# Batch 0's last tokens of k and v: loads to 128 partitions, k spread by head with a mask

One core of a Trainium2 chip. The metric is the device time of one execution in microseconds (us), lower is better. Times in the text count from the start of the profiled execution. In lines of the profile, PE is TensorE (PEld its loads of weights), DVE is VectorE, ACT is ScalarE, POOL is GpSimd and SP is SyncE; L873 is line 873 of that kernel; "the chain of work that ended last" is followed back from the last instruction, at each step to what released it. A pair is two heads; pair 2 is heads 4 and 5.

## The reference

A linear attention without softmax, a norm, and then a gated feed-forward layer with a residual. Cut to what matters here:

```python
# q, k, v: [8 batches, 8 heads, 576 tokens, 64]
kv = np.einsum('bhsd,bhse->bhde', k, v)          # a sum over all 576 tokens
out = np.einsum('bhsd,bhde->bhse', q, kv)
rms = np.sqrt(np.mean(out * out, axis=-1, keepdims=True) + 1e-06)
x = out / rms * g_norm                           # to [4608 tokens, 512]
# then, for all tokens: gelu(x @ w_gate) * (x @ w_val) @ w_out, gated, plus x
```

The sum over tokens is what the change uses: k and v rows of a token may sit on any partition, as long as both sit on the same one. 576 tokens are 512 (4 on each of 128 partitions) and 64 last ones.

## The kernel before, the parts concerned

Batch 0 has to be loaded before anything can run. Its fp32 rows come over SyncE's queue, half of the heads at a time; tiles that are used later serve as landing places (`th_all` for the last tokens).

```python
def load_first_last(half):                        # last tokens of k and v, 4 heads
    hs = slice(half * HH, (half + 1) * HH)        # HH = 4
    for i, t in enumerate((k, v)):
        nc.sync.dma_start(
            out=first_raw[i][half][0 : R // 2, :].rearrange("p (h x) -> p h x", h=HH),   # 32 partitions
            in_=t[0, hs, M0:S, :].rearrange("h (p j) d -> p h (j d)", j=2),
        )
# order of the queue: q k | last k, last v | v (heads 0-3), q k (4,5) | last k, last v | v (4,5), q k v (6,7), weights
...
for t in first_last:
    nc.vector.memset(t, 0.0)                      # partitions 32 to 127 stay zero
...
def f_cast_last(i, half, copy):                   # fp32 to fp16, 32 x 512
    hs = slice(half * HH, (half + 1) * HH)
    copy(
        out=first_last[i].rearrange("p j h d -> p h j d")[0 : R // 2, hs, :, :],
        in_=first_raw[i][half][0 : R // 2, :].rearrange("p (h j d) -> p h j d", h=HH, j=2),
    )
...
def f_kv(pr):                                     # kv of a pair of heads, 128 x 128
    for j in range(NJ):
        nc.tensor.matmul(ps, lhsT=k16[:, j, cs], rhs=b16_t[0, "v"][...], start=(j == 0), stop=False)
    for j in range(2):
        kl, vl = (t[:, j].rearrange("p h d -> p (h d)")[:, cs] for t in first_last)
        nc.tensor.matmul(ps, lhsT=kl, rhs=vl, start=False, stop=(j == 1))
...
# the opening, in order; the last letter is the engine (A ScalarE, D VectorE, P GpSimd).
# kc, vc, qc: casts; lk, lv: casts of last tokens; kv: f_kv; kvo: its mask product;
# warm3: three matmuls of zeros that keep TensorE's clock up
opening = """
qc1P qc0A qT1 qT0 kc1P kc0A qo0D warm3 lv0D lk0P qo1A warm3 vc1D vc0A kv1 qc2A kv0 kvo1 kvo0 o1 kc2P qT2
lk1P lv1D sq1 qo2D o0 warm3 warm2 vc2P sq0 rd1 kv2 qc3P rt1 kvo2 rd0 ...
"""
```

## Time and profile before

| | before |
|---|---|
| time, median of 3 runs | 338.99 us (338.89 to 339.11) |
| span of the profiled execution | 337.3 us |
| TensorE busy | 326.6 us, 97% of the span |
| 512-byte packets of SyncE's queue in the opening | 512, all of them last tokens |
| v of heads 4 and 5 landed | 11.70 us |
| mask product of kv, pair 2, started | 12.95 us |
| first gelu started | 22.68 us |

TensorE is full from the first gelu on, so the table's last three rows are the whole case: a landing, the product that waits for it, and the point from which the rest has a fixed length (337.35 - 22.68 = 314.67 us; it is 314.61 to 314.67 us in all fourteen profiles of this case). "Landed" is the last of the sixteen completion increments that the trace holds for a transfer. The lines that carry this reading are in the prediction.

### The profile page before, as it was taken

How to read it: one execution, taken by the hardware profiler on the slowest of the kernel's cores; microseconds unless marked ns; L12 is line 12 of the kernel's file. 1: busy time of each engine (PE TensorE's matmuls, PEld its weight loads, DVE VectorE, ACT ScalarE, POOL GpSimd, SP SyncE). 2: the span in 40 equal slices, each digit the busy share in tenths (PEclk: the TensorE clock that was granted, in tenths of full speed). 3: DMA queues.
4: the chain of work that ended last, by engine and by line, in shares of the span. 5: the costliest groups of instructions: out<-in, count | busy, mean ns of one | idle time of the engine just before them, and what ended most of it. 6: DMA issues, size and time to landing. Idle time of an engine off the chain costs nothing.

```text
span 337.3 us, 6523 instructions
## 1 busy us (share of the span) xinstructions
PE 326.6 (97%) x2576; PEld 200.9 (60%) x2576; DVE 255.4 (76%) x498; ACT 161.5 (48%) x289; POOL 109.3 (32%) x127
## 2 busy tenths in 40 slices
PE   8889999999999999999999999999999999999993
PEld 3444454444844476447644674458444888788872
DVE  6755449669859988788677968796789877777754
ACT  3663384264335361536163535343454376646760
POOL 2783161990053108400650057003200251142232
PEclk9999999999999999999999999999999999999998
DMA  8999999669489272983498339924300330011004
GB/s 239 319 197 204 195 203 158 171 101 151 83 134 171 105 115 104 174 85 77 135 176 94 63 102 179 136 45 98 126 0 5 74 125 2 2 54 73 0 2 124
DMA packets 76688, 38.82 MB, mean 115 GB/s; under 512 B 42098, under 2 KB 74354, under 8 KB 76658
## 3 DMA queue, kind: packets, MB, share of 16 engines
q0 software_dynamic: 38752, 17.17, 40.4%
q1 hardware_dynamic: 37328, 20.71, 22.4%
q10 hardware_dynamic: 578, 0.52, 0.5%
q8 instruction: 20, 0.33, 0.4%
q14 instruction: 10, 0.08, 0.1%
HBM read 38.80 MB, written 9.44 MB: 143 GB/s over the span
## 4 chain that ended last, share of the span: by engine, by line
PE 90%; DVE 4%; DMA 3%; issue 0%; ACT 0%; POOL 0%; SPq 0%; DVEq 0%
PE gps L357 21%; PE vps L357 20%; PE wA L452 11%; PE rps L377 8%; PE fps L394 3%; PE Av L692 3%; PE Ag L692 3%; PE wE L452 3%; PE wD L452 3%; PE wF L452 3%; PE w L452 2%; DMA hid_s<-in_v_dram 2%; PE kvp L208 2%; PE Fv L692 2%; PE Fg L692 2%; DMA kf<-in_k_dram 2%
## 5 line engine op out<-in xcount | busy, mean ns | idle before, releaser
L345 ACT ACTIVATE ge<-gps 128x512 f16<-128x512 f32 x84 | 50.2, 598 | 98.4 <-PE gps L357 96.7
L357 PE MATMUL vps<-xT,wv 128*128 128x512 f16 x328 | 84.2, 379 | 0.8 <-DVE hid L346 0.8
L357 PE MATMUL gps<-xT,wg 128*128 128x512 f16 x328 | 84.3, 380 | 0.0
L346 DVE TENSOR_TENSOR hid<-ge,vps 128x512 f16<-128x512 f16 x84 | 57.4, 684 | 32.6 <-PE vps L357 28.7
L492 POOL TENSOR_TENSOR osb<-osb,t 128x512 f32<-128x512 f32 x28 | 35.3, 1277 | 138.0 <-DVE osb L488 132.4
L357 PEld LDWEIGHTS <-wv 128*128 128x128 f16 x328 | 32.1, 98 | 39.7 <-issue 1.1
L357 PEld LDWEIGHTS <-wg 128*128 128x128 f16 x328 | 30.7, 98 | 34.5 <-issue 0.2
L452 PEld LDWEIGHTS <-hid_s 128*128 128x128 f16 x384 | 37.6, 98 | 4.5 <-issue 0.2
L377 PE MATMUL rps<-wr,xT 128*128 128x512 f16 x144 | 32.5, 379 | 0.0
L452 PEld LDWEIGHTS <-hid 128*128 128x128 f16 x288 | 28.2, 98 | 5.5 <-issue 0.8
L386 ACT ACTIVATE th<-rps 128x512 f32<-128x512 f32 x36 | 21.5, 599 | 16.4 <-PE rps L377 16.4
L377 PEld LDWEIGHTS <-xT 128*128 128x128 f16 x144 | 14.1, 98 | 16.6
L245 DVE TENSOR_REDUCE ss<-sq 128x8 f32<-128x512 f32 x32 | 20.6, 680 | 2.9 <-ACT sq L243 2.8
L452 PE MATMUL wA<-wo_ts,hid_s 128*128 128x256 f16 x168 | 20.6, 273 | 0.0
L692 PEld LDWEIGHTS <-ws 128*128 128x128 f16 x192 | 18.8, 98 | 2.2
L391 ACT ACTIVATE th<-th 128x512 f32<-128x512 f32 x36 | 19.9, 623 | 0.0
L303 DVE TENSOR_TENSOR t<-op,ny 128x512 f16<-128x512 f32 x28 | 17.9, 685 | 0.1
L243 ACT ACTIVATE sq<-op 128x512 f32<-128x512 f32 x28 | 15.3, 598 | 4.5 <-PE op L226 4.1
L317 DVE TENSOR_TENSOR t<-t,g 128x512 f16<-128x512 f16 x36 | 15.4, 478 | 0.1
L425 DVE TENSOR_TENSOR hid_s<-hid 128x1536 f16<-128x1536 f16 x16 | 15.3, 954 | 0.2
L729 POOL TENSOR_TENSOR hid<-ge,c 128x512 f16<-128x512 f16 x6 | 7.0, 1163 | 23.4 <-ACT ge L723 23.4
L394 PE MATMUL fps<-wo,hid 128*128 128x512 f16 x48 | 11.2, 379 | 0.0
(172 smaller groups left out, 472.5 us busy)
## 6 DMA issues: line engine op xcount, KB each, us to landing
out_dram<-osb SPq DMA_DIRECT2D x14, 512.0 KB, 2.6
qraw<-in_q_dram POOLq DMA_DIRECT2D x7, 512.0 KB, 8.1
k<-in_k_dram POOLq DMA_DIRECT2D x7, 512.0 KB, 9.7
v<-in_v_dram POOLq DMA_DIRECT2D x7, 512.0 KB, 11.5
wg<-in_moe_w_gate_dram POOLq DMA_DIRECT2D x2, 512.0 KB, 8.2
wv<-in_moe_w_val_dram POOLq DMA_DIRECT2D x2, 512.0 KB, 9.0
wo<-in_moe_w_out_dram POOLq DMA_DIRECT2D x2, 512.0 KB, 13.6
out_dram<-osb SPq DMA_DIRECT2D x4, 256.0 KB, 2.9
```

Source lines behind the costliest of these rows:

```text
L245: nc.vector.tensor_reduce(out=out_, in_=sq, op=ALU.add, axis=mybir.AxisListType.X)
L303: nc.vector.tensor_tensor(out=t, in0=o, in1=scale, op=ALU.mult)
L345: nc.scalar.activation(out=ge, in_=gps, func=AF.Gelu)
L346: nc.vector.tensor_tensor(out=hids[blk][:, f, :], in0=ge, in1=vps, op=ALU.mult)
L357: nc.tensor.matmul(ps[:, j0 * P : j1 * P], lhsT=w[:, cc, :], rhs=xT_t[blk][:, j0:j1, cc, :], start=(cc == 0 and j0 == 0), stop=(cc == NP - ...
L377: nc.tensor.matmul(rps, lhsT=xT_t[blk][:, j, cc, :], rhs=wr16[:, cc, :], start=(cc == 0), stop=(cc == NP - 1),)
L386: nc.scalar.activation(out=th, in_=rps, func=AF.Tanh, scale=0.5)
L391: nc.scalar.activation(out=th, in_=th, func=AF.Copy, scale=0.5, bias=0.5)
L394: nc.tensor.matmul(fps, lhsT=hids[blk][:, f, j * P : (j + 1) * P], rhs=wo16[:, f, :], start=(f == 0), stop=(f == NF - 1))
L452: nc.tensor.matmul(ps[:, e - es[0], :], lhsT=a[:, f, e * P : (e + 1) * P], rhs=b[:, f, :], start=(start and e == es[0] and f == 0), stop=( ...
L492: nc.gpsimd.tensor_tensor(out=res_all[of], in0=res_all[of], in1=t_t[blk][of], op=ALU.add)
L692: nc.tensor.matmul(out_[:, r, :], lhsT=lhsT, rhs=rhs, start=(first and r == 0 and c == 0), stop=(c == 1), skip_group_check=True,)
```

## The change

Intent: load each pair of last rows to all 128 partitions, one head's two tokens (512 bytes) on each, instead of to 32 partitions with four heads on each. A row then belongs to head (partition mod 4). For k it is spread to four heads' columns and multiplied by a mask of rows (`of_head`, 1 where the row belongs to the head), so every matmul still sums only its own head's rows; v is copied twice, once for each head of a pair. The memsets of partitions 32 to 127 are no longer needed.

```diff
--- before.py
+++ after.py
@@ -789,14 +789,18 @@
     first_raw, first_last = [], []
     for which in "kv":
         t = hid_of[which]
-        first_last.append(t[:, 2 * H * NJ * D :][:, 0 : 2 * H * D].rearrange("p (j h d) -> p j h d", j=2, h=H))
-        first_raw.append([th_all[:, 2 * len(first_raw) + i, :] for i in range(2)])
+        rest = t[:, 2 * H * NJ * D :]
+        if which == "k":
+            first_last.append(rest[:, 0 : 2 * H * D].rearrange("p (j h d) -> p j h d", j=2, h=H))
+        else:
+            first_last.append(rest[:, 0 : 8 * D].rearrange("p (i j e d) -> p i j e d", i=2, j=2, e=2))
+        first_raw.append([th_all[:, 2 * len(first_raw) + i, 0 : 2 * D] for i in range(2)])
 
     def load_first_last(half):
         hs = slice(half * HH, (half + 1) * HH)
         for i, t in enumerate((k, v)):
             nc.sync.dma_start(
-                out=first_raw[i][half][0 : R // 2, :].rearrange("p (h x) -> p h x", h=HH),
+                out=first_raw[i][half],
                 in_=t[0, hs, M0:S, :].rearrange("h (p j) d -> p h (j d)", j=2),
             )
 
@@ -823,8 +827,6 @@
 
     zeros = consts.tile([P, C], FP16, name="zeros")
     nc.vector.memset(zeros, 0.0)
-    for t in first_last:
-        nc.vector.memset(t, 0.0)
     mask = consts.tile([P, P], FP32, name="mask")
     nc.vector.memset(mask, 0.0)
     nc.vector.memset(mask[0:D, 0:D], 1.0)
@@ -837,6 +839,10 @@
     nc.vector.memset(one32, 1.0)
     ident = consts.tile([P, P], FP16, name="ident")
     nc.vector.tensor_copy(out=ident, in_=ident32)
+    of_head = consts.tile([P, HH], FP32, name="of_head")
+    nc.vector.tensor_reduce(
+        out=of_head, in_=ident32.rearrange("p (r h) -> p h r", h=HH), op=ALU.add, axis=mybir.AxisListType.X
+    )
     grow32 = consts.tile([1, 2, D], FP32, name="grow32")
     nc.vector.tensor_copy(out=grow32, in_=grow[:, None, :].to_broadcast([1, 2, D]))
     grow16 = consts.tile([1, H, D], FP16, name="grow16")
@@ -877,12 +883,20 @@
                 in_=src.rearrange("p h (j d) -> p h j d", j=NJ)[:, hs, :, :],
             )
 
-    def f_cast_last(i, half, copy):
-        hs = slice(half * HH, (half + 1) * HH)
-        copy(
-            out=first_last[i].rearrange("p j h d -> p h j d")[0 : R // 2, hs, :, :],
-            in_=first_raw[i][half][0 : R // 2, :].rearrange("p (h j d) -> p h j d", h=HH, j=2),
-        )
+    def f_k_last(half, engs):
+
+        raw_ = first_raw[0][half].rearrange("p (j d) -> p j d", j=2)
+        for j, eng in enumerate(engs):
+            eng.tensor_tensor(
+                out=first_last[0][:, j, half * HH : (half + 1) * HH, :],
+                in0=raw_[:, j, None, :].to_broadcast([P, HH, D]),
+                in1=of_head[:, :, None].to_broadcast([P, HH, D]),
+                op=ALU.mult,
+            )
+
+    def f_v_last(half, copy):
+        raw_ = first_raw[1][half].rearrange("p (j d) -> p j d", j=2)
+        copy(out=first_last[1][:, half], in_=raw_[:, :, None, :].to_broadcast([P, 2, 2, D]))
 
     def f_qT(pr):
         q16 = b16_t[0, "q"].rearrange("p j h d -> p j (h d)")
@@ -903,7 +917,8 @@
                 ps, lhsT=k16[:, j, cs], rhs=b16_t[0, "v"][:, hs, j * D : (j + 1) * D], start=(j == 0), stop=False
             )
         for j in range(2):
-            kl, vl = (t[:, j].rearrange("p h d -> p (h d)")[:, cs] for t in first_last)
+            kl = first_last[0][:, j].rearrange("p h d -> p (h d)")[:, cs]
+            vl = first_last[1][:, pr // 2, j].rearrange("p e d -> p (e d)")
             nc.tensor.matmul(ps, lhsT=kl, rhs=vl, start=False, stop=(j == 1))
 
     def f_kv_out(pr):
@@ -981,8 +996,10 @@
         eng = rest[-1:]
         if name in ("qc", "kc", "vc"):
             f_cast(name[0], pr, engines[eng])
-        elif name in ("lk", "lv"):
-            f_cast_last("kv".index(name[1]), pr, engines[eng])
+        elif name == "lk":
+            f_k_last(pr, (nc.gpsimd if eng == "P" else nc.vector, nc.vector))
+        elif name == "lv":
+            f_v_last(pr, engines[eng])
         elif name == "warm":
             keep_warm(pr)
         elif name == "wg":
@@ -1022,8 +1039,8 @@
 
 
     opening = """
-    qc1P qc0A qT1 qT0 kc1P kc0A qo0D warm3 lv0D lk0P qo1A warm3 vc1D vc0A kv1 qc2A kv0 kvo1 kvo0 o1 kc2P qT2
-    lk1P lv1D sq1 qo2D o0 warm3 warm2 vc2P sq0 rd1 kv2 qc3P rt1 kvo2 rd0 kc3A qT3 wg1 wv1 ri1 o2 rt0 t1 warm3 warm1 sq2 vc3D
+    qc1P qc0A qT1 qT0 kc1P kc0A qo0D warm3 lk0D lv0P qo1A warm3 vc1D vc0A kv1 qc2A kv0 kvo1 kvo0 o1 kc2P qT2
+    lk1P sq1 qo2D o0 warm3 warm2 vc2P sq0 lv1A rd1 kv2 qc3P rt1 kvo2 rd0 kc3A qT3 wg1 wv1 ri1 o2 rt0 t1 warm3 warm1 sq2 vc3D
     rd2 qo3A xT1 kv3 wg2 wcg0P rt2 kvo3 ri0 ri2 warm2 o3 t2 xo1A wcg1P sq3a wcv0P sq3b g1 xT2 rd3a wcv1P rd3b
     wv2 t0 xo2A wg3 wv3 v1 xT0 rt3 ri3 xo0A g2 v2 t3a t3b xT3a xT3b g0 xo3aA xo3bD gelu v0 g3a v3a g3b v3b
     """
```

The prediction was made with this diff, the order of instructions that it builds to, and the profile of the kernel before.

> **What bounds the kernel now.** I read the page first, then the chain of work that ended last, then the transfers in stretches of time, then the timeline of the first 24 us. The page says where there is anything to win: TensorE is busy in nine tenths or more of every slice but the first three and the last (a slice is 8.4 us).
>
> ```profile
> PE   8889999999999999999999999999999999999993
> ```
>
> So only the opening, batch 0's attention up to about 22 us, can give time, and from there the work of TensorE simply follows: in the chain, TensorE runs without a gap above 0.03 us from 20.90 us through all the batches that I looked at (to 83 us). Whatever the opening gains should shift everything after it. In the opening the chain (start, length, what) runs through transfers:
>
> ```profile
> 1.27 5.13 DMA kf<-in_k_dram
> 6.40 0.02 issue
> 6.42 5.28 DMA hid_s<-in_v_dram
> 11.70 0.05 issue
> 11.75 0.62 POOL v L873
> 12.38 0.04 issue
> 12.42 0.38 PE kvp L902 x4
> 12.80 0.13 PE kvp L907 x2
> 12.93 0.02 issue
> 12.95 0.29 DVE kv L910
> 13.24 0.59 DVE ss L927
> ```
>
> The landing of v for heads 4 and 5 at 11.70 us sets it: GpSimd casts it, TensorE forms kv of pair 2, VectorE masks it, and from 12.95 us VectorE then works almost without a break to 18.19 us. So the question is when that v lands. It is the tenth transfer of one queue: q, k, last k, last v, v of heads 0 to 3, q, k of heads 4 and 5, last k, last v of heads 4 to 7, and then it. The transfers' view of four stretches (packets, bytes, mean rate; 5.50 to 7.00 us, 7.00 to 8.50, 9.25 to 11.00, 11.00 to 13.00) shows a queue that is busy throughout but moves half as much in two of them:
>
> ```profile
> DMA packets 376, 0.32 MB, mean 213 GB/s; under 512 B 18, under 2 KB 376, under 8 KB 376
> ```
> ```profile
> DMA packets 583, 0.57 MB, mean 379 GB/s; under 512 B 28, under 2 KB 583, under 8 KB 583
> ```
> ```profile
> DMA packets 456, 0.38 MB, mean 219 GB/s; under 512 B 32, under 2 KB 456, under 8 KB 456
> ```
> ```profile
> DMA packets 793, 0.76 MB, mean 382 GB/s; under 512 B 47, under 2 KB 793, under 8 KB 793
> ```
>
> The 512-byte packets are those of the last tokens. Each slow stretch begins when a pair of them has been started (4.75 to 6.2 us and 8.5 to 10 us by packet starts), and goes on into v's ordinary 1 KB packets, whose median rises from 46 ns to about 86 ns. v of heads 6 and 7, of the same form but behind no such pair, runs at full rate. The loss is 1.50 x (1 - 213/379) = 0.66 us and 1.75 x (1 - 219/382) = 0.75 us: 1.4 us in all, all ahead of the 11.70 us landing.
>
> **What the Trainium skill says.** "SBUF — State Buffer", section "Door 1: The DMA port swizzle", says that a transfer's rate depends on how many of 16 memory ports its partitions reach, and that partitions 0 to 31 reach 8, all 128 reach 16. The loads of last tokens go to partitions 0 to 31. The trace agrees in kind: 213 against 379 GB/s. It doesn't agree in amount: 128 KB at half rate would lose 128/200 - 128/380 = 0.3 us, an estimate from the two rates, where the trace loses 0.66 to 0.75. The congestion outlives the narrow packets. "DMA: Bandwidth & Descriptors", section "Why a DMA increments its semaphore by 16 and not by 1", says that the number of engines is the largest up to 16 that divides the slowest dimensions of both sides. That is 16 for 32 rows too, and the trace has sixteen completion increments for each narrow load, for the first from 5.80 to 6.96 us. So I read the words "over 16 engines" as no change of engines: if anything is won, it is from the partitions. "SBUF — State Buffer", section "Who interferes with whom", says that a VectorE instruction with two inputs in SBUF contends with a GpSimd instruction that reads SBUF. The new products are such; the kernel before has no test of it in this stage.
>
> **The change part by part.** Bytes, packets (512 B) and engines stay; only the destination's partitions change.
>
> 1. Transfers, on the path. If the slow stretches go, v of heads 0 to 3 lands 0.7 us earlier (8.49 to 7.8), v of heads 4 and 5 1.4 us earlier (11.70 to about 10.3), and k, v of heads 6 and 7 and the two weight pieces likewise.
>
> 2. Issues, beside. The queue's issues took 0.33 to 0.51 us each. The built program no longer gives the four narrow loads the mark of quick issue that they had; of unmarked issues of this queue the trace has four stores (L558), 0.60 to 0.73 us. So some 0.2 us more each: v of heads 0 to 3 would be issued at about 3.3 us instead of 2.82. Its packets need not begin before 5.5, and the first transfer went from issue (0.74) to first packets (about 1.8) in 1.1 us, so this is covered.
>
> 3. VectorE's first stage, beside. Two memsets of 0.48 us go, one reduction of 128x128 comes, about 0.25 us (the cast of that shape took 0.21). VectorE then waited 1.18 us for the transposes anyway: nothing gained.
>
> ```profile
> 1.19 0.48 DVE L827 MEMSET kf<- 128x512 uint32 x1
> ...
> 7.08 0.60 POOL L882 CAST kf<-th 32x512 f16<-32x512 f32 x1
> ...
> 7.44 0.52 DVE L882 CAST hid_s<-th 32x512 f16<-32x512 f32 x1 [0.27 <-DMA th<-in_v_dram]
> ...
> 10.93 0.60 POOL L882 CAST kf<-th 32x512 f16<-32x512 f32 x1
> ...
> 11.30 0.51 DVE L882 CAST hid_s<-th 32x512 f16<-32x512 f32 x1 [1.17 <-DMA th<-in_v_dram]
> ```
>
> 4. First half. One VectorE cast (0.52) and one GpSimd cast (0.60) become two products of 128x256 on VectorE and one spread copy of 128x256 on GpSimd. A VectorE product with 128x256 results takes 0.42 us (L941, 128x256 form), so some 0.38 each, 0.76 together; the copy about 0.35 (half of the 0.61 of 128x512, and a little). The products follow the copy of qT (ends 7.17) and end at about 7.95; the v cast follows, to 8.4 instead of 8.92. TensorE's keep-warm matmuls run to about 8.6 and hold kv of pair 1 there as well: it starts at 8.5 rather than 8.97. Of the 0.7 us that v wins here, about 0.45 arrives.
>
> 5. Second half. GpSimd's cast (0.60) becomes a product of half the elements (the 128x512 sum of L492 took 1.28, so about 0.65). VectorE's cast becomes one product (0.38), and v's copy moves to ScalarE (about 0.38, as its 128x256 square took). On ScalarE it stands behind two squares, which end about 0.45 earlier than 11.36, at 10.9; so it is done at 11.3. GpSimd casts v from 10.3 to 10.95. TensorE leaves its keep-warm matmuls at about 11.15. kv of pair 2 thus starts at about 11.15 and ends at 11.6 (before: 12.42 and 12.93), and its mask product starts at 11.7 instead of 12.95: 1.2 us won. VectorE has its qT copy and first reduction done by 11.1, so it isn't the bound there.
>
> 6. After that. VectorE's run from 12.95 to 18.19 us keeps its order and shifts. What it meets has moved as well: v of heads 6 and 7, the weight pieces, and the weights that GpSimd fetches from 12.95 us on, as its preceding work ends earlier. The weights of the later columns land some us ahead of their use, so TensorE doesn't meet a new wait.
>
> Sum: -1.2 us if the slow stretches vanish, of which nothing is lost later. 338.99 - 1.2 = 337.8.
>
> **The rivals.**
> (a) The slow stretches aren't from the 32 partitions but from the source, 16 KB per head read by all engines at once, or from 512-byte packets as such. Both stay as they are. Against it: the v packets behind the pair, with an ordinary source, are slow for almost a microsecond after the last narrow packet started, which looks like writes backing up. For it: the loss is twice what ports alone would give. Then v lands at 11.70 as before, the products are covered, and the time is 338.9 to 339.1.
> (b) The stretches only shrink. Each engine probably gets two source rows, hence eight neighbouring partitions, so at each moment several engines may still crowd one port. Half the gain, 338.4.
> (c) A new bound takes over: ScalarE's copy of v standing ahead of kv of pair 2, VectorE's two products ahead of the v cast, or products stretched by GpSimd's reads. Each adds 0.3 to 0.4 us where the transfers are early; it turns -1.2 into -0.8, 338.2. With (a) it gives 339.1 to 339.3.
> (d) The slower issues starve the engines: 0.2 to 0.5 us per pair, if descriptors of the changed form come late. Against it is the slack of about 2 us in part 2.
>
> **Range and chances.** I give the full mechanism about 55 in 100 (337.5 to 337.9), (b) and (c) some 25 (338.0 to 338.5), (a) and (d) some 20 (338.9 to 339.3). The middle of this is 337.9; eight in ten lie between 337.4 and 339.0. Two per cent are 6.8 us. The opening has 22 us, and the change touches under 2 us of its path, so neither limit is in reach: within 2% has 0.98.
>
> **What would show it.** Right: no stretch near 210 GB/s before 13 us; v of heads 4 and 5 landing at about 10.3; kv of pair 2 at about 11.2; the first gelu group (L345) at about 21.5 instead of 22.68; the rest of the span as long as before. Products near 0.38 us, narrow issues of 0.6 to 0.7 us. Wrong: slow stretches as before (the source, or packet size); early landings but a late kv of pair 2 with a wait on ScalarE or VectorE ahead of it (rival c); idle transfer engines between 5 and 10 us (rival d); or an opening that gains and a later wait of TensorE on weights that gives it back.

## The result

| | before | after |
|---|---|---|
| time, median of 4 runs | 339.05 us (338.89 to 339.24) | 338.48 us (338.47 to 338.61) |
| span of the profiled execution | 337.3 us | 336.6 us |
| v of heads 4 and 5 landed | 11.70 us | 10.85 us |
| mask product of kv, pair 2, started | 12.95 us | 12.22 us |
| first gelu started | 22.68 us | 21.94 us |

The result is correct, and 0.57 us shorter: ratio 0.9984, 95% interval 0.9967 to 1.0001. A ratio here is the mean time of one kernel's fast runs over that of the other's of the same rounds, so not quite the ratio of the medians. The change is too small for this interval to exclude that it does nothing, but the profiles agree with it. The intervals of two later measurements lie wholly below 1: the changed kernel again (e6_after_again) and, in the third group, the changed kernel with one tile padded (e10_pad64). What the opening won (0.73 us at the mask product, 0.74 us at the first gelu) stands to the end: 336.55 - 21.94 = 314.61 us is the same rest as before, to 0.05 us.

The transfers' view of the changed kernel, for three of the stretches that the prediction shows (5.50 to 7.00 us, 9.25 to 11.00, 11.00 to 13.00):

```profile
DMA packets 562, 0.51 MB, mean 338 GB/s; under 512 B 21, under 2 KB 562, under 8 KB 562
```
```profile
DMA packets 633, 0.60 MB, mean 341 GB/s; under 512 B 36, under 2 KB 633, under 8 KB 633
```
```profile
DMA packets 716, 0.70 MB, mean 350 GB/s; under 512 B 33, under 2 KB 716, under 8 KB 716
```

The slow stretches are gone: 338 and 341 GB/s where 213 and 219 were. But the third line was 382 before. The queue now runs a tenth slower everywhere behind the first loads of last tokens; its 1 KB packets take 51 ns in the median, where they took 46 outside the slow stretches. The chain of work that ended last, in the changed kernel (start, length, what):

```profile
4.33 5.34 DMA kf<-in_k_dram
...
9.72 0.22 POOL k L881
9.93 0.36 issue
10.30 0.78 POOL kf L890
11.08 0.57 POOL v L879
...
11.69 0.38 PE kvp L916 x4
...
12.22 0.29 DVE kv L925
```

It no longer goes through the landing of v at 10.85 us but through the one of k of heads 4 and 5 (9.67) and three pieces of GpSimd behind it: the cast of k, the new product for the last k (L890), the cast of v. So two things stand between the predicted 11.7 us and the measured 12.22: slower packets, and a GpSimd that is 0.2 us late. The timeline shows why the products of the second half were longer than I took them to be:

```profile
7.09 0.75 DVE L890 TENSOR_TENSOR kf<-th,of_head 128x256 f16<-128x256 f32 x2
...
9.72 0.62 POOL L881 CAST k<-kf 128x512 f16<-128x512 f32 x1 [2.49 <-DMA kf<-in_k_dram]
9.92 0.69 DVE L890 TENSOR_TENSOR kf<-th,of_head 128x256 f16<-128x256 f32 x1
...
10.30 0.78 POOL L890 TENSOR_TENSOR kf<-th,of_head 128x256 f16<-128x256 f32 x1
```

The two products at 7.09 us take 0.375 us each (0.75 for both), mostly with GpSimd idle. The one at 9.92 takes 0.69: it falls into GpSimd's cast of k. If VectorE waits until that cast ends (10.34) and then needs its 0.375, it ends at 10.7; it ended at 10.61. This is the contention that the Trainium skill states for a VectorE instruction with two inputs in memory against a GpSimd one that reads it ("SBUF — State Buffer", section "Who interferes with whom"). It struck whichever came second. Here GpSimd's product began while VectorE's was still running, and took 0.78 us. In e6_after_again, the same kernel again, GpSimd's began first and took 0.62; there VectorE's took 0.81, and ended 0.28 us after GpSimd's:

```profile
10.18 0.62 POOL L890 TENSOR_TENSOR kf<-th,of_head 128x256 f16<-128x256 f32 x1
10.27 0.81 DVE L890 TENSOR_TENSOR kf<-th,of_head 128x256 f16<-128x256 f32 x1
```

VectorE was free in time all the same: its mask product of pair 2 waited for TensorE (0.68 us), so on the chain only GpSimd's part counts.

### The profile page after: what moved, and what is told of

Its sections match the earlier page's. It is cut to its first block, busy times and chain, and to the rows that moved or that the text cites. A ratio compares the mean times of both kernels' runs of the same rounds, so it can differ in the third digit from the quotient of the medians.

```text
span 336.6 us, 6522 instructions
## 1 busy us (share of the span) xinstructions
PE 326.7 (97%) x2576; PEld 200.9 (60%) x2576; DVE 255.1 (76%) x498; ACT 161.5 (48%) x290; POOL 109.4 (33%) x127
## 4 chain that ended last, share of the span: by engine, by line
PE 91%; DVE 4%; DMA 2%; SPq 1%; issue 1%; POOL 0%; ACT 0%; DVEq 0%
PE gps L357 21%; PE vps L357 21%; PE wA L452 11%; PE rps L377 8%; PE fps L394 3%; PE Av L692 3%; PE Ag L692 3%; PE wF L452 3%; PE wE L452 3%; PE wD L452 3%; PE w L452 2%; DMA kf<-in_k_dram 2%; PE kvp L208 2%; PE Fg L692 2%; PE Fv L692 2%; PE op L226 1%
## 5 line engine op out<-in xcount | busy, mean ns | idle before, releaser
L386 ACT ACTIVATE th<-rps 128x512 f32<-128x512 f32 x36 | 21.5, 598 | 16.4 <-PE rps L377 16.4
```

The costliest lines, as they stand in the source:

```text
L386: nc.scalar.activation(out=th, in_=rps, func=AF.Tanh, scale=0.5)
```

## The experiments

Theory: the 32 partitions cause the slow stretches, and taking these away is the whole gain. Rivals: the gain comes of the new arithmetic (products, fewer memsets), or of the slower form of issue. Then two questions that the result opened: what makes packets slower, and what holds the opening now. Twelve kernels ran, in three groups of four; the first two groups on one chip, the third on another. Runs in the slow state (over 1.5% above the fastest of the same kernel; here one of the kernel before, 344.84 us) are left out of ratios.

### 1. The transfers alone (e1_dst128)

The kernel before, with only the destination changed. The casts keep engine, number and size; they read one head's 512 bytes four times over, so the result is wrong on purpose.

```diff
-                out=first_raw[i][half][0 : R // 2, :].rearrange("p (h x) -> p h x", h=HH),
+                out=first_raw[i][half][:, 0 : 2 * D],
...
-            in_=first_raw[i][half][0 : R // 2, :].rearrange("p (h j d) -> p h j d", h=HH, j=2),
+            in_=first_raw[i][half][0 : R // 2, 0 : 2 * D].rearrange("p (j d) -> p j d", j=2)[:, None, :, :].to_broadcast([R // 2, HH, 2, D]),
```

> The kernel before with nothing changed but the destination of the four loads of last tokens: 128 partitions of 512 bytes instead of 32 of 2 KB. The casts stay as they were in number, engine and size (they read one partition's 512 bytes four times over, so the result is wrong on purpose). If the partitions are the cause of the two slow stretches, both vanish as in the changed kernel (about 340 GB/s instead of 213 and 219), v of heads 4 and 5 lands near 10.9 us instead of 11.70, its cast on GpSimd starts near 11.0, the mask product of pair 2 near 12.1 to 12.2, and the time is 338.4 to 338.5, the whole gain of the change. If the gain came from the changed arithmetic (products, copies, memsets taken away), the time stays at 338.9 to 339.1 whatever the transfers do.

Measured, transfers from 5.50 to 7.00 us and from 9.25 to 11.00:

```profile
DMA packets 617, 0.57 MB, mean 377 GB/s; under 512 B 29, under 2 KB 617, under 8 KB 617
```
```profile
DMA packets 690, 0.66 MB, mean 378 GB/s; under 512 B 44, under 2 KB 690, under 8 KB 690
```

No slow stretch, and full-speed packets (46 ns). v of heads 4 and 5 landed at 10.26 us, against a predicted 10.3 for the changed kernel (and 10.9 expected here, after the changed kernel's profile), and the mask product started at 11.79, against a predicted 11.7:

```profile
11.79 0.29 DVE L910 TENSOR_TENSOR kv<-kvp,mask 128x128 f16<-128x128 f32 x1 [0.68 <-PE kvp L907]
```

So the destination alone does what the prediction gave to the whole change, and more than the whole change did (12.22). By times this batch decides nothing: 338.54 us (338.03 to 342.78, 6 runs) against 339.59 (338.67 to 344.84, 11 runs), ratio 0.9983, interval 0.9935 to 1.0031. The kernel before scattered on this chip; experiment 4 shows one such execution.

### 2. The form of issue (e2_form)

The kernel before, correct, its four narrow loads kept from the quick form of issue, the destination unchanged.

```diff
+        nc.dge_precook = False
         for i, t in enumerate((k, v)):
             nc.sync.dma_start(
...
+        nc.dge_precook = True
```

> The kernel before, right result, with the four loads of last tokens to 32 partitions as before but issued in the slower form that the changed kernel's loads have (the mark of quick issue withheld). Theory of the partitions: each of these issues takes about 0.6 us instead of 0.33 to 0.50, the slow stretches stay (near 215 GB/s), v of heads 4 and 5 lands at 11.7, and the time stays at 338.9 to 339.2. Rival, that it is the form or the later issue that keeps the queue from congesting: the stretches vanish here too and the time falls to about 338.5. Side question: whether packets of 1 KB take 51 ns instead of 46 after such loads, as in the changed kernel; if so that comes of the form.

Measured, same two stretches:

```profile
DMA packets 415, 0.37 MB, mean 248 GB/s; under 512 B 16, under 2 KB 415, under 8 KB 415
```
```profile
DMA packets 503, 0.46 MB, mean 263 GB/s; under 512 B 29, under 2 KB 503, under 8 KB 503
```

The slow stretches stay. They are milder than 213 and 219, but not milder than those of the kernel before on this chip (254 and 279, experiment 4). The four issues in this form took 0.59 to 0.76 us, v landed at 11.32, and the time was 339.06 us (338.67 to 339.45). The form costs nothing that shows, and isn't what helps. It isn't what slows the packets either: 46 ns.

### 3. Which 32 partitions, and 64 (e3_32apart, e9_64low)

Two variants of the kernel before, both wrong on purpose. The first puts the rows on 32 partitions four apart; the second on the 64 neighbours 0 to 63. The cut shows the destinations alone: e3 has four clearing memsets on GpSimd as well, e9 casts that fit its rows, and both the slower form of issue.

```diff
-                out=first_raw[i][half][0 : R // 2, :].rearrange("p (h x) -> p h x", h=HH),
+                out=first_raw[i][half].rearrange("(p s) (h x) -> p s h x", s=4, h=HH)[:, 0],      # e3
+                out=first_raw[i][half][0:R, 0 : 4 * D],                                           # e9
```

> The kernel before with the loads of last tokens put on 32 partitions four apart (0, 4, ... 124) instead of 32 neighbours; packets, rows per partition and the slower issue form included; GpSimd clears the tiles first, in its idle time; the casts read partitions 0 to 31 as before (wrong result on purpose). If the cause is which memory ports the partitions reach, these 32 reach all 16 and the slow stretches vanish: no 1 KB packets near 86 ns, v of heads 4 and 5 near 10.9 us, time 338.4 to 338.6. If it is the number of partitions, or four rows going to one partition, the stretches stay at about 215 GB/s and the time at 338.9 to 339.2.

> The kernel before with the loads of last tokens on the 64 neighbouring partitions 0 to 63, 1 KB each (the casts read 32 of them, wrong result on purpose). By the skill's map of memory ports, partitions 0 to 63 reach the same 8 ports as 0 to 31, so the slow stretches should stay much as they were (200 to 250 GB/s for 1 us or more, v of heads 4 and 5 near 11.3 to 11.7). If it is the number of partitions that counts, they shrink to about half, or vanish. Time 338.7 to 339.1 by the ports.

Measured from 5.50 to 7.00 us, first 32 partitions four apart, then 64 neighbours:

```profile
DMA packets 617, 0.57 MB, mean 380 GB/s; under 512 B 25, under 2 KB 617, under 8 KB 617
```
```profile
DMA packets 376, 0.34 MB, mean 228 GB/s; under 512 B 11, under 2 KB 376, under 8 KB 376
```

32 partitions suffice if they are spread, and 64 don't if they are neighbours from 0 on. In the second stretch the spread ones had 324 GB/s with a median of 46 ns (a few single packets of up to 0.55 us in it, none of the broad slowing), the 64 neighbours 243 GB/s. v of heads 4 and 5 landed at 10.15 and at 11.49 us. That is what the Trainium skill's map of ports says ("SBUF — State Buffer", section "Door 1: The DMA port swizzle"): 0 to 63 reach the same 8 of 16 as 0 to 31. The number of partitions, the rows per partition and the packet size don't explain it; the set of partitions does.

By times, 338.63 us (338.50 to 339.07, 4 runs) and 339.13 (338.74 to 339.80, 4 runs). The spread one expected 338.4 to 338.6 and lost some of its early landing: its profiled execution had the mask product only at 12.46 us. Experiment 7 is about why.

### 4. Both kernels again (e6_after_again, e7_before_again)

Unchanged copies, on the chip of the first group.

> The changed kernel, unchanged, on another chip and beside the kernel before again. Question: its 1 KB packets took 51 ns (345 GB/s) after the loads of last tokens, where the transfer-only version with the very same loads had 46 ns (382 GB/s) throughout. If that belongs to the changed kernel, it is there again; if it varies from execution to execution, it need not be. Second question: the full TensorE clock was granted at 8.43 us here and between 7.81 and 9.57 us in the other profiles; kv of pair 1 started with the end of the keep-warm matmuls, so I expect its start to follow that instant (about 0.35 us behind it when the grant comes after 8.1 us). Time 338.3 to 338.6.

> The kernel before, once more with a profile, on the chip of these runs. If the slow stretches are its own, they are there again: two of about 1.5 us at 200 to 250 GB/s, v of heads 4 and 5 at 11.3 to 11.7 us, against a version of the quick or slow issue form, which had 11.32. If they were a chance of one execution, they are missing.

The changed kernel: 338.40 us (338.35 to 338.64, 6 runs), packets at 49 ns, v landed at 10.73. Beside the kernel before of the two groups (12 runs, 339.3 in the median; 339.0 without the slow one), the ratio is 0.9962 (0.9928 to 0.9995). The ratio counts the long runs of the kernel before that aren't slow by the rule (up to 341.94 us), so it flatters the change. Its slower packets are its own, then, not a chance of one execution: on this chip five versions of the kernel before had 46 ns, and three of the changed kernel 49 or 51. One expectation was a miss: kv of pair 1 started at 9.06 us, ahead of the full clock (9.31) and not 0.35 behind it.

The kernel before: slow stretches again, 254 and 279 GB/s, as expected. But this execution took 340.31 us (a single run, so its state is unknown), and v of heads 4 and 5 landed at 12.54, outside what I expected. The completion increments show where: fifteen of the sixteen for v of heads 0 to 3 had come by 8.20 us, the sixteenth at 10.02, so one engine lagged. It did so from the first last k on (fifteen by 6.65, the sixteenth at 8.12). One 512-byte packet of 0.64 us stands at 5.81, but the trace doesn't name its engine, and it is shorter than the lag. From one such profile I can't say what makes an engine fall behind, nor that the change mends it (one of six runs of e1_dst128 took 342.78 us). So the kernel before's long runs on this chip are not counted as a gain of the change.

### 5. GpSimd's product moved, and v's copy brought forward (e5_k_dve, e8_v_first)

```diff
-    lk1P sq1 qo2D o0 warm3 warm2 vc2P sq0 lv1A rd1 ...
+    lk1D sq1 qo2D o0 warm3 warm2 vc2P sq0 lv1A rd1 ...          # e5
+    lk1D lv1A sq1 qo2D o0 warm3 warm2 vc2P sq0 rd1 ...          # e8
```

> The changed kernel with both products of the second half's k on VectorE, none on GpSimd. In the changed kernel the chain goes through GpSimd's cast of k (9.72), its product (10.30, 0.78 us) and then its cast of v (11.03, while v landed at 10.85). With the product gone, the cast of v starts on the landing, at about 10.9, kv of pair 2 at about 11.55 instead of 11.69, and the mask product near 12.05 instead of 12.22: 0.15 to 0.2 us off the changed kernel. Rival: VectorE's products wait while GpSimd's cast of k reads memory (its one product took 0.69 us there instead of 0.38), so two of them, the copy of qT and the reduction end at about 12.2 and nothing is gained.

> The changed kernel with both products of the second k on VectorE and the second copy of v on ScalarE moved ahead of the two squares. With the products moved alone, kv of pair 2 waited for GpSimd's cast (to 11.35) and then for ScalarE's copy, which stood behind the squares (11.12 to 11.53), and was masked at 12.01. Ahead of the squares the copy runs as it lands (9.9 to 10.35), so the mask product should start near 11.85, 0.15 us less again, if the squares (0.2 us later) do not become the bound through the reduction. Time 0.1 to 0.2 below the version with the products moved, 338.0 to 338.1. Rival: the delayed squares delay the first reduction and square root by as much, and nothing is won.

With both products on VectorE, the cast of v followed its landing (10.74 against 10.69), and the mask product started at 12.01 instead of 12.22 (12.35 in the second profile of the changed kernel): 0.2 us, as expected. Both products together took 0.84 us, part of it in GpSimd's cast, and VectorE was free in time. 338.18 us (338.12 to 338.57, 6 runs), ratio to the kernel before of its batch 0.9957 (0.9927 to 0.9988); against 338.40 of the changed kernel on the same chip, in another batch, 0.2 us less. Within a batch the times don't confirm this: the next version, which has the moved product too, took 338.47 us beside those 338.40, and e12_pad_k_dve 338.47 beside 338.52 of e10_pad64. So the 0.2 us is shown at the mask product, in single profiles, and not by times.

Bringing v's copy forward was a miss: mask product at 11.99, and 338.47 us (338.15 to 339.08). TensorE began kv of pair 2 at 11.46 us, with the end of GpSimd's cast, as it had in e5_k_dve (11.47), and then needs 0.53 us to the mask product. ScalarE's copy, which I took for the bound, had been ready in time in both.

### 6. The tile that moved the others (e10_pad64, e11_dst128_by32, e12_pad_k_dve)

The new tile `of_head` moves every tile behind it by 32 bytes, landing places included. First a mend (64 bytes), then the converse (32 bytes put into e1_dst128), and the mend together with the moved product.

```diff
-    of_head = consts.tile([P, HH], FP32, name="of_head")
+    of_head = consts.tile([P, 16], FP32, name="of_head")[:, 0:HH]      # e10 and e12
...
+    pad = consts.tile([P, 4], FP32, name="pad")                        # e11, in e1_dst128
+    nc.vector.memset(pad, 0.0)
```

> The changed kernel with its new tile of four numbers per partition (of_head) given 64 bytes instead of the 32 that it takes. In the changed kernel that tile moved every tile behind it by 32 bytes, so that none of the loads' destinations starts at a multiple of 64 bytes any more; in all four profiles with it 1 KB packets take 49 to 51 ns after the first loads of last tokens, in all six without it 46. If the alignment is the cause, they take 46 ns here (about 380 GB/s), v of heads 4 and 5 lands near 10.3 us instead of 10.7 to 10.85, the mask product of pair 2 starts near 11.9 to 12.0 (then after ScalarE's copy of v), and the time is 0.2 to 0.3 below the changed kernel: 338.1 to 338.3. If the slower packets come from the arithmetic (products, fewer memsets), they stay at 49 to 51 and the time at 338.4 to 338.5.

> The converse: the transfer-only version (old casts, 128 partitions, wrong result on purpose), which had 46 ns throughout, with a tile of 32 bytes put ahead of the others and cleared once. If the alignment is the cause, its 1 KB packets take 49 to 51 ns from the first loads of last tokens on, v of heads 4 and 5 lands near 10.75 instead of 10.26, and the time rises by about 0.4 us to that of the changed kernel (338.4 to 338.6). If not, nothing changes (46 ns, 10.26).

> The changed kernel with the 64 bytes and with both second products of k on VectorE: the two mends together. v lands near 10.3 and its cast on GpSimd no longer waits for a product, but kv of pair 2 then waits for ScalarE's copy of v behind the squares (to about 11.4 to 11.5), so over the 64 bytes alone I expect no more than 0.1 us: 338.0 to 338.2.

The mend failed: 51 ns, v landed at 10.82, 338.52 us (338.43 to 339.12). The converse came as expected; its transfers from 11.00 to 13.00 us, where e1_dst128 had 373 GB/s:

```profile
DMA packets 713, 0.70 MB, mean 349 GB/s; under 512 B 32, under 2 KB 713, under 8 KB 713
```

51 ns, v at 10.74, 338.56 us (338.39 to 339.04, 5 runs). A multiple of 64 bytes is therefore not enough. It could be the place as such: in the kernel before, the places for q and v start at multiples of 256 bytes, and neither shift keeps that. But the two answers came from the other chip, where no version with the old places was profiled. Either the places do it, or the new arithmetic on one chip and something of the other chip on the other. The traces set a limit to the places as well. In every version with moved places, packets of the first q and k, which go to moved places too, take 46 ns in the median until about 4.5 us; only from the first loads of last tokens on do packets take longer. And in e1_dst128 the place for k starts 64 bytes past a multiple of 256 (by the built program's addresses), and they take 46 ns throughout. So a moved place alone doesn't slow a packet, nor do the new loads alone; in these runs the slowing shows only where both are present. What slows the packets stays open; only the theory "a multiple of 64 restores it" has fallen.

e11_dst128_by32 bears on another point. It has the changed kernel's transfers at their slower rate and none of its arithmetic, and takes 338.56 us beside 338.52 of the changed kernel with 64 bytes, on the same chip; both beat the kernel before of that batch (339.07 us, 338.89 to 339.67, 9 runs), with ratios 0.9985 (0.9972 to 0.9997) and 0.9983 (0.9969 to 0.9996). So the new loads make the gain without the new arithmetic, which is there to make the loads usable. What the arithmetic adds or takes is too small for these times: the medians differ by 0.04 us, and each version's five runs spread over 0.65 to 0.7. e12_pad_k_dve: mask product at 12.04, as in e5_k_dve (12.01), since the places gave nothing; 338.47 us (338.17 to 338.94), ratio 0.9978 (0.9966 to 0.9991).

### 7. The keep-warm matmuls (e13_fewer_warm)

In profiles with an early v, kv of pair 1 started at quite different times, 8.45 to 9.21 us. The six matmuls of zeros ahead of it are the same in all; their lines in the timelines of e8_v_first, the changed kernel and e6_after_again (start, length):

```profile
6.50 1.87 PE L858 MATMUL idle<-zeros 128*128 128x512 f16 x6
```
```profile
6.51 2.41 PE L858 MATMUL idle<-zeros 128*128 128x512 f16 x6
```
```profile
6.50 2.77 PE L858 MATMUL idle<-zeros 128*128 128x512 f16 x6
```

The trace's first record of TensorE's full clock is at 7.32, 8.43 and 9.31 us in these three. Until then a matmul of 512 columns starts every 0.43 us, later every 0.22. The Trainium skill says so: the clock is gated to half until TensorE has been busy for one window of about 3.4 us, and the window runs freely, so the instant differs from run to run ("TensorE: Matmul & The Clock Gate", section "Part 1: The HAM clock gate"). It names a spread of 0.5 us either way; the fourteen profiles here have 7.32 to 10.10 us. In the profile of the kernel before this didn't matter, as the clock came at 7.83, v landed at 8.47 and was cast by 8.92. It is no matter of the new loads alone: in e2_form, with the old destination, v was cast by 8.71, and with the clock at 9.57 kv of pair 1 started at 9.06. With v at 7.7 to 8.2 the matmuls of zeros are what kv of pair 1 waits for whenever the clock comes late. The last experiment drops two of them, on top of e12_pad_k_dve.

```diff
-    qc1P qc0A qT1 qT0 kc1P kc0A qo0D warm3 lk0D lv0P qo1A warm3 vc1D vc0A kv1 ...
+    qc1P qc0A qT1 qT0 kc1P kc0A qo0D warm3 lk0D lv0P qo1A warm1 vc1D vc0A kv1 ...
```

> As the version with both mends, and the last group of keep-warm matmuls ahead of kv of pair 1 cut from three to one. With the full clock granted at 8.4 us or later these matmuls ended only at 8.7 to 9.2 us and held kv of pair 1, whose v was cast by 8.5. If they are the bound, kv of pair 1 starts at about 8.4 whatever the grant, the squares and ScalarE's copy of v come up to 0.5 us earlier, the mask product of pair 2 starts near 11.7, and the time falls by 0.1 to 0.3 us to 337.8 to 338.0. Rival: with fewer of them the full clock comes later, and the matmuls and transposes until then run slower: no gain or a loss.

The profiled execution had a late clock, 9.79 us. Its keep-warm matmuls and kv of pair 1 in the timeline, and then those of e10_pad64 with nearly the same instant (9.88):

```profile
6.50 1.91 PE L858 MATMUL idle<-zeros 128*128 128x512 f16 x4
8.62 0.59 PE L916 MATMUL kvp<-v,k 128*128 128x128 f16 x4 [0.21 <-DVE v L879]
```
```profile
6.50 2.77 PE L858 MATMUL idle<-zeros 128*128 128x512 f16 x6
9.06 0.63 PE L916 MATMUL kvp<-v,k 128*128 128x128 f16 x4
```

kv of pair 1 now waits for v, not for zeros, 0.44 us earlier, and the mask product of pair 2 starts at 12.21 instead of 12.57. That compares two kernels that differ in the moved product too (0.2 us). It does not reach the 11.7 that I expected, nor the time the 337.8 to 338.0: at half clock, kv itself is slow, and v had landed at 8.12. 338.33 us (338.18 to 338.47, 5 runs), ratio 0.9974 (0.9961 to 0.9986). Beside e12_pad_k_dve (338.47 us) the median is 0.14 lower, and the spread is 0.3 us instead of 0.8. With five runs that is a hint, not a verdict. The rival, a later clock for want of matmuls, isn't excluded: 9.79 us is the third latest of the fourteen, from one profile.

### All in one table

Times in us. "Full clock" is the trace's first record of it; "1 KB" is the median time of a 1 KB packet of SyncE's queue from 10.9 to 13.5 us; n is the number of runs.

| version | full clock | kv pair 1 | v 4, 5 landed | mask pair 2 | first gelu | 1 KB, ns | median (n) |
|---|---|---|---|---|---|---|---|
| before | 7.83 | 8.97 | 11.70 | 12.95 | 22.68 | 46 | 339.05 (4) |
| after | 8.43 | 8.76 | 10.85 | 12.22 | 21.94 | 51 | 338.48 (4) |
| e1_dst128 | 7.81 | 8.45 | 10.26 | 11.79 | 21.5 | 46 | 338.54 (6) |
| e2_form | 9.57 | 9.06 | 11.32 | 12.57 | 22.3 | 46 | 339.06 (6) |
| e3_32apart | 9.37 | 9.21 | 10.15 | 12.46 | 22.5 | 46 | 338.63 (4) |
| e5_k_dve | 8.62 | 8.85 | 10.69 | 12.01 | 21.7 | 51 | 338.18 (6) |
| e6_after_again | 9.31 | 9.06 | 10.73 | 12.35 | 22.1 | 49 | 338.40 (6) |
| e7_before_again | 9.11 | 10.53 | 12.54 | 14.03 | 23.8 | 46 | 340.31 (1) |
| e8_v_first | 7.32 | 8.53 | 10.74 | 11.99 | 21.7 | 51 | 338.47 (6) |
| e9_64low | 7.45 | 8.82 | 11.49 | 12.74 | 22.5 | 46 | 339.13 (4) |
| e10_pad64 | 9.88 | 9.06 | 10.82 | 12.57 | 22.5 | 51 | 338.52 (5) |
| e11_dst128_by32 | 10.10 | 9.07 | 10.74 | 12.62 | 22.5 | 51 | 338.56 (5) |
| e12_pad_k_dve | 8.68 | 8.88 | 10.78 | 12.04 | 21.8 | 51 | 338.47 (5) |
| e13_fewer_warm | 9.79 | 8.62 | 10.78 | 12.21 | 21.9 | 51 | 338.33 (5) |

## Why the prediction was right, and where it was not

The range held (337.4 to 339.0; measured 338.48), the change stayed within 2%, and the mechanism is shown: spread destinations, no slow stretches, an earlier v, and a gain that lasts to the end. The size was half: 0.57 us by the times and 0.73 at the mask product, where the sum said 1.2. The measured time lies not in the 337.5 to 337.9 of the full mechanism, which had 55 in 100, but in the 338.0 to 338.5 of (b) and (c), which had 25: the range held because it allowed for half the gain. By its parts:

- **Part 1, transfers.** Right in kind, too large in size. "v of heads 4 and 5 1.4 us earlier" was 0.85. The estimate took for granted that the queue would run at the 380 GB/s of its undisturbed stretches; in the changed kernel it runs at 338 to 350. Where the queue did run at 380, in e1_dst128, the landing was 10.26 against the 10.3 of the estimate. I find nothing in the profile of before that told this, and its cause is open.
- **Part 2, issues.** Right: 0.55 to 0.67 us each, and covered, as e2_form shows by itself.
- **Part 3, VectorE's first stage.** Right in effect. The reduction took 0.36 us, not 0.25; VectorE then waited 1.55 us for the transposes instead of 1.18.
- **Part 4, first half.** The products took the 0.38 us that I gave them. kv of pair 1 came at 8.76 instead of 8.5. I had noted that keep-warm matmuls hold it "to about 8.6" (and yet wrote 8.5), but read that as a fixed time; it moves with the clock by some 0.9 us (their group takes 1.87 to 2.77 us).
- **Part 5, second half.** GpSimd's product took 0.78 us instead of 0.65, and VectorE's 0.69 instead of 0.38. I named that contention as rival (c), but left it out of the sum; without an overlap 0.65 would have done (0.62 in e6_after_again). "GpSimd casts v from 10.3" became 11.03: 0.55 us of it the later landing, 0.18 the product ahead of it. Moving the product away gave 0.2 us back at the mask product (e5_k_dve).
- **Part 6, after that.** Right: the rest is 314.67 and 314.61 us.

Of the rivals, (a) and (d) fell (e1_dst128, e3_32apart, e9_64low, e2_form). (b) named the right number, 338.4, for a reason that did not hold: the stretches vanished, and the loss is spread over all later packets. (c) holds for GpSimd's product, which VectorE's stretched, worth 0.2 us at the mask product; not for ScalarE's copy (e8_v_first), and not for VectorE's own products, which ended in time.

What stays open: what raises the 1 KB packet from 46 to 51 ns, which goes with about 0.5 us of landing (10.26 against 10.69 to 10.85); and why the slow stretches cost twice what half the ports would.

## What to carry to other kernels

A small transfer to few partitions can slow the large ones queued behind it, long after its own last packet: look at the rate in short stretches, not at the small transfer's own time, and choose partitions that spread over the memory's ports rather than merely more of them. When a landing comes earlier, check what was hidden behind the old one: here a product on a busy engine, and a run of filler matmuls whose length depends on when the clock rises. Time differences of 0.2% are decided better by the instants of one chain in the trace than by medians, but an instant is one execution's, so look for what moves it from run to run: here everything after the first gelu took the same 314.61 to 314.67 us in fourteen profiles, and all that differed lay ahead of it.

## What the Trainium skill lacked or had wrong

- "SBUF — State Buffer", section "Door 1: The DMA port swizzle": its map of ports predicted all four destinations right (0 to 31 and 0 to 63 slow, 213 and 228 GB/s; four apart and all 128 fast, 380 and 377). It lacks that loads queued behind a narrow one are slowed too: 1 KB packets went from 46 to a median of 81 to 86 ns, for about a microsecond after the last narrow packet started, and the loss was 0.66 to 0.75 us per 128 KB, where half the ports account for 0.3. "DMA: Bandwidth & Descriptors" tells of such back-pressure, but for copies between cores, and without a figure.
- "TensorE: Matmul & The Clock Gate", section "Part 1: The HAM clock gate": a free-running window fits, but the instant of the full clock spread over 2.8 us here (7.32 to 10.10), more than the 0.5 us either way that it names, with the same matmuls ahead of it in all profiles but e13_fewer_warm's. (The same section also has one kernel with 6, 11 or 14 slow matmuls, which comes nearer.)
- No page that I read has the quick and the slow form of issue on SyncE's queue: 0.33 to 0.51 us in the kernel before, 0.55 to 0.67 us for the unmarked loads of the changed kernel (0.59 for a marked one right behind two of them); which of the two a load gets is settled when the program is built.
- No page that I read explains a 1 KB packet going from 46 to 51 ns with the landing places moved by 32 or 64 bytes. "DMA: Bandwidth & Descriptors" counts extra work for a start off a multiple of 256 bytes, but moved places took 46 ns here until about 4.5 us; the cause is not settled.
